# A layer of attention and gated FFN on one core: the softmax exponentials shared out anew between ScalarE and VectorE

## Chip, cores and metric

The kernel runs on one core of one Trainium2 chip. The metric is the device time of one execution in microseconds (us). Three runs of the kernel before gave 913.15, 915.69 and 915.77, a median of 915.69. One more execution was profiled. Where a statement rests on the profile, it is of that execution alone.

## What is computed

For x of 2048 rows and 640 columns: a layer norm, an attention with 32 heads of 20 columns without a mask, a residual, a second layer norm, a gated FFN of width 1728, and a second residual. Cut to what matters:

```python
def _A_ref(x, wqkv, wo):
    qkv = (x @ wqkv).reshape(B, S, 3, H, Dh).transpose(2, 0, 3, 1, 4)
    q, k, v = qkv[0], qkv[1], qkv[2]
    scores = jnp.einsum("bhqd,bhkd->bhqk", q, k) * (Dh ** -0.5)
    p = _softmax(scores, axis=-1)
    o = jnp.einsum("bhqk,bhkd->bhqd", p, v)
    return o.transpose(0, 2, 1, 3).reshape(B, S, D) @ wo

def _B_ref(x, w_gate, w_up, w_down):
    h = _gelu(x @ w_gate) * (x @ w_up)
    return h @ w_down

h  = x + _A_ref(_layernorm(x), A_wqkv, A_wo)
h2 = h + _B_ref(_layernorm(h), B_w_gate, B_w_up, B_w_down)
```

The scores are 32 x 2048 x 2048 numbers, and each needs one exponential.

## The kernel before

**Tiles, quads, slots.** A score tile is 128 keys by 512 queries' worth of one head (for chunks of fewer queries, several blocks of keys side by side), one bank of PSUM. Four heads stand in the four row groups of TensorE, so four tiles of the same keys make a quad. The queries are cut into eight chunks (CHUNKS) of 512, five times 256 and twice 128. A slot is 16 quads (64 tiles) of one chunk: chunk 0 has slots 0 to 7, chunks 1 to 5 have four slots each (8 to 27), chunks 6 and 7 two each (28 to 31). So there are 32 slots with 2048 tiles.

**Two engines for the exponential.** Most tiles go to ScalarE: units of alternately three and two tiles (PAT) are written by TensorE (score matmuls, L965), one ACTIVATE with the function Exp reads a unit from PSUM and writes its probabilities to a ring of 18 tiles (pts holds 12, pts2 in rege 6; both are the groups with line L368 on ACT). D_QUADS says, slot by slot, how many quads are computed by VectorE instead (d_exp): for each tile one TENSOR_SCALAR out of PSUM (L889), and then, for two tiles together (narrow, 128x1024) before slot D_WIDE = 18 and four together (wide, 128x2048) from there on, four operations that form a correction polynomial, a DMA issued by GpSimd that adds the correction into the tile (the slots in DA_SLOTS), and a last TENSOR_SCALAR. D_LEAD says how many ScalarE tiles ahead of its place in the slot a VectorE tile is begun.

**What follows a quad.** TensorE multiplies the probabilities with the values (PV, `ps<-pts,v_all` and like groups), adding up a slot in PSUM bank 6. The last PV of a slot waits for the slot's VectorE quads; then `osb` takes the sums out of the bank, and the next slot's PV begins there. ScalarE can't write a place of the ring before the PV that read it is done.

**Work between.** While the attention of chunk c + 1 runs, the output projection, the second layer norm and the FFN of chunk c (post, down) run in the gaps: L667 with wo, L1138 gate and up, L1218 down. DMA transposes on SyncE (dma_transposes) turn the normalised rows. The gelu of a chunk is on ScalarE, with a table load before and after. After the last Exp comes the tail: what is left of chunk 6, and all of chunk 7 after its attention.

**What sets the order.** The program is not written in its final order: `op` records operations with a planned duration, a latency after it (`lat`, for a DMA the time until it lands), a priority and dependencies. `Sched.schedule` then plays a list schedule and fixes the order of each engine's instructions; `emit` writes them with semaphore waits. Matmuls with zeros (`ps<-kt_all,zer`) are put in where the plan finds TensorE little used. So a changed count or latency moves instructions on all engines, though the work is the same. The constants in question:

```python
DA_ISSUE, DA_LAT = 0.95, 7.0
D_QUADS = (1,) + (2,) * 15 + (2, 2) + (3,) * 10 + (2, 2, 2, 2)
D_LEAD = ((0,) * 8, (0, 10, 20) + (42,) * 21)
D_WIDE = 18
```

Of the kernel before, what the change touches and what calls it, by code (L numbers as in the profile page):

```python
# [46 lines left out]
class Sched:  # L47
# [13 lines left out]
    def op(self, eng, fns, dur, prio, reads=(), writes=(), acq=(), rel=(), after=(), sem=None, lat=None, mode=None, util=0.0):  # L61
        if eng == "dve" and rel and prio > self.ev:
            prio = self.ev
        o = Op()
        o.i = len(self.ops)
        o.eng, o.dur, o.lat, o.sem = eng, dur, DRAIN[eng] if lat is None else lat, sem
        o.util = util
        o.mode = mode
        o.tag = writes[0] if writes else None
        o.fns = fns if isinstance(fns, list) else [fns]  # L70
        o.prio = (prio, o.i)
        deps = set(after)
        for r in reads:
            if r in self.lw:
                deps.add(self.lw[r])
        for w in writes:
            if w in self.lw:
                deps.add(self.lw[w])
            deps.update(self.rd.get(w, ()))
        for r in reads:  # L80
            self.rd.setdefault(r, []).append(o.i)
        for w in writes:
            self.lw[w] = o.i
            self.rd[w] = []
        deps.discard(o.i)
        o.deps = deps
        o.acq = list(acq)
        o.rel = list(rel)
        o.succ = []
        o.ready = 0.0  # L90
        self.ops.append(o)
        return o.i
# [237 lines left out]
PV_QUADS = 2  # L330
D_LAG = 8
MERGE = (1,)
DA_ISSUE, DA_LAT = 0.95, 7.0
DA_SLOTS = (1, 2, 3, 5) + tuple(range(9, 32))
PR, PR2 = 12, 6
D_QUADS = (1,) + (2,) * 15 + (2, 2) + (3,) * 10 + (2, 2, 2, 2)
D_FIRST, D_PART = 2, 0.75
D_LEAD = ((0,) * 8, (0, 10, 20) + (42,) * 21)
D_WIDE = 18
RSQRT_MAGIC = float(0x5F3759DF)  # L340

# [1 line left out]
P_QK, P_PV, P_PRO, P_EPI, P_LN, P_BG = 0, 1, 1.5, 2, 2.5, 3  # L343
# [3 lines left out]
def bass_sequential_preLN__mha_block__glu_gated_geglu__prompt_kernel(  # L347
# [12 lines left out]
    with ExitStack() as es:  # L360
        sc = Sched(nc)
        op = sc.op
# [4 lines left out]
        def I(method, *args, **kwargs):  # L367
            return lambda eng: getattr(eng, method)(*args, **kwargs)  # L368
# [64 lines left out]
        wg = carve(NA * DFF).rearrange("p (a f) -> p a f", a=NA)  # L433
        wu = carve(NA * DFF).rearrange("p (a f) -> p a f", a=NA)
# [55 lines left out]
        def cst(fn, key, n=128):  # L490
# [7 lines left out]
           reads=["zer"], writes=["qf1"])  # L498
        op("act", I("activation", f32(qt_all[:, 2, :, :]), zer[:, 0:2].bitcast(FP32).to_broadcast([128, 2048]), ACT.Copy), 1.8, P_QK,
           reads=["zer"], writes=["qf2"])  # L500
        op("act", I("activation", v_all[:, :, :, DH], zer[:, 0:1].unsqueeze(2).to_broadcast([128, NT, H]), ACT.Copy, bias=1.0), 0.5, P_QK,
           reads=["zer"], writes=["vones"])
# [28 lines left out]
        def load(dst, src, key, mb, after=(), writes=None):  # L531
            return op("sp", I("dma_start", dst, src), 0.08, P_BG, writes=writes or [key], after=after,
                      sem=key, lat=mb)
# [85 lines left out]
                   rel=[bk], after=after)  # L619

        def dma_transposes(src, rkeys, dst, wkey, after=()):
            op("sp", I("dma_start_transpose", dst, src), 1.25, P_EPI, reads=rkeys, writes=[wkey], sem=f"xp{wkey[1]}", lat=2.0, after=after)

        _id = [0]

# [114 lines left out]
        def proj_q(t, c, banks, prio, evac="dve"):  # L740
            proj_qk(0, t, c, q_un[:, t, :], ("qu", t), banks, prio, evac)
            if t == 0 and c == 0:
                for j in range(4):
                    q_keys[0][0].append(("q", 0, 0, j))
                    dma(qt_all[32 * j + 1:32 * j + 21, 0, 0, :], q_un[DH * j:DH * j + DH, 0, :], ("q", 0, 0, j),
                        [("qu", 0), "qtm0"], "qc", 2.2, prio - 0.1)
            dma(qdr[c, 128 * t:128 * t + 128, :], q_un[:, t, :], ("qdr", c, t), [("qu", t)], f"qw{t}", 2.7,
                max(prio, P_BG) if t == 0 else prio, 0.4)
            w_readers.append(op("dve", I("tensor_scalar", aq[t].bitcast(I16), q_un[:, t, :].bitcast(I16), 0x7FFF, None,
                                         ALU.bitwise_and), 0.2, prio, reads=[("qu", t)], writes=[aqk(t)]))  # L750

        def q_bound(c, ts, g0, g1, banks, prio):
            bk = Bank(*banks)
            key = ("bk", sc_id())
            for k, t in enumerate(ts):
                w_readers.append(op("pe", lambda eng, k=k, t=t: eng.matmul(
                    bank(bk)[0:32, :], sel[:, t, :], aq[t], start=(k == 0), stop=(k == len(ts) - 1)),
                    c_mm(512), prio, mode="full", util=0.05, reads=[aqk(t), ("sel", t)], writes=[key],
                    acq=[bk] if k == 0 else []))
            op("dve", lambda eng: eng.tensor_scalar(qoff[0:32, :], bank(bk)[0:32, :], OFF, None, ALU.add), c_dve(512), prio,  # L760
               reads=[key], writes=["qoff"], rel=[bk])
            dma(odr[c], qoff[0:32, :], ("odr", c, g0), ["qoff"], "ow", 2.5, prio, 0.4)
            new = [("qo", c, g0)] + [("q", c, g0, j) for j in range(4)]
            for j in range(4):
                dma(qt_all[32 * j + 1:32 * j + 21, c, g0:g1, :],
                    qdr[c].rearrange("(g j e) s -> j e g s", j=4, e=DH)[j, :, g0:g1, :], ("q", c, g0, j),
                    [("qdr", c, t) for t in ts] + q_fills[c], f"q{c}{g0}", 2.5, prio, keep=False)
            dma(qt_all[0:128:32, c, g0:g1, :], odr[c].rearrange("(g j) s -> j g s", j=4)[:, g0:g1, :], ("qo", c, g0),
                [("odr", c, g0)] + q_fills[c], f"q{c}{g0}", 2.5, prio, keep=False)
            for g in range(g0, g1):  # L770
                q_keys[g][c] += new
# [36 lines left out]
        slot_end = []  # L808
        lead = sum(D_LEAD, ())
        for s_, (c, gs) in enumerate(slots):  # L810
            nk = 512 // CHUNKS[c][1]
            quads = [(s_, g, kb) for g in gs for kb in range(NT // nk)]
            n = D_QUADS[s_]
            taken = [quads[len(quads) * (m + 1) // (n + 1)] for m in range(n)]
# [258 lines left out]
        def prefetch(c):  # L1073
            q0, nq = CHUNKS[c]
            nt = nq // 128
            tb = base(c)
            op("sp", I("dma_start", h_sb[:, tb:tb + nt, :], x_hbm[q0:q0 + nq, :].rearrange("(t p) d -> p t d", p=128)), 0.08, P_EPI,
               writes=[("h", tb + tt, hf) for tt in range(nt) for hf in range(2)], sem=f"xr{c}", lat=2.0 + nq * 0.0034,
               after=tuple(e_ops) + tuple(w_readers) if c == 0 else ())
# [167 lines left out]
        for s_, (c, gs) in enumerate(slots):  # L1247
            if c == 0:
                g = s_
                if g + 1 in STEP:  # L1250
                    t, (g0, g1) = g + 1, STEP[g + 1]
                    pr = P_EPI if t == 1 else P_BG
                    proj_q(t, 0, BG0, pr)
                    proj_k(t, BG0, pr)
                    q_bound(0, (t - 1, t), g0, g1, BG0, pr)
                if g < 3:
                    for kt in range(NT * g // 3, NT * (g + 1) // 3):
                        proj_v(kt, 1, BG0, P_BG)
                if g == 5:
                    prefetch(0)  # L1260
                if g >= 5:
                    cc = g - 4
                    for t in range(NA):
                        proj_q(t, cc, BG0, P_BG)
                    q_bound(cc, tuple(range(NA)), 0, NG, BG0, P_BG)
                if g == 7:
                    wr = tuple(w_readers)
                    load(wg, B_w_gate.rearrange("(a p) f -> p a f", p=128), "wg", 11.0, after=wr)
                    load(wu, B_w_up.rearrange("(a p) f -> p a f", p=128), "wu", 16.0, after=wr)
                    load(wd[:, 0:NF - 1, :], B_w_down[0:(NF - 1) * 128, :].rearrange("(a p) d -> p a d", p=128),  # L1270
                         "wd", 21.0, after=wr)
                    r0 = (NF - 1) * 128 - F0[-1]
                    load(wd[r0:128, NF - 1, :], B_w_down[(NF - 1) * 128:DFF, :], "wd", 2.6, after=wr)
                    op(POOL, I("memset", wd[0:r0, NF - 1, :], 0.0), 0.8, P_BG, writes=["wdz", "pool"], after=wr)
            while ui < len(units) and begins[ui] < slot_end[s_]:
                unit(ui)
                ui += 1
            if gs[-1] == NG - 1:
                tail = c == len(CHUNKS) - 1
                sc.ev = P_EV  # L1280
                post(c, ALLB if tail else BGF[c + 1], ALLB if tail else BGC[c + 1], tail)
                if not tail:
                    prefetch(c + 1)
# [30 lines left out]
```

## Time and profile before

| | us |
|---|---|
| device time, median of three | 915.69 |
| device time of the profiled execution | 915.13 |
| its span (first to last instruction) | 913.0 |
| ACT (ScalarE) busy | 871.2 |
| PE (TensorE) busy | 832.7 |
| DVE (VectorE) busy | 763.3 |
| POOL (GpSimd) busy | 134.2 |
| first and last Exp start | 32.9 and 875.2 |

The first 33 us are the loads, the first layer norm and the first projections; 33 to 876 us is the stretch of the exponentials, and the rest is the tail. Busy times overlap each other and an engine that is off the critical path may be busy or idle at no cost, so the table must be read with the chain of waits and, for each stage, with the windows. PE's busy time says little, since matmuls are pipelined and counted to their modelled end.

### The profile page before, as it was taken

What the parts mean: (1) busy time and instruction counts of PE and PEld (TensorE: products, weight loads), DVE (VectorE), ACT (ScalarE), POOL (GpSimd) and SP (SyncE); (2) the same over time, 40 slices, a digit from 0 to 9 for tenths busy, and PEclk for the clock granted to TensorE, in tenths of its full rate; (3) what the DMA queues carried; (4) which work ended last, traced back from release to release, by engine and by line L of the source; (5) the groups of instructions that cost most, each with busy time, mean ns of one, the idle gap of its engine ahead of it and who ended that gap; (6) DMA issues with size and microseconds to landing.
All of it is one profiled execution on the core that took longest, in us unless ns stands there. A gap on an engine that the chain in (4) does not pass through costs nothing.

```text
span 913.0 us, 25152 instructions
## 1 busy us (share of the span) xinstructions
PE 832.7 (91%) x11135; PEld 383.4 (42%) x11180; DVE 763.3 (84%) x1426; ACT 871.2 (95%) x786; POOL 134.2 (15%) x239
## 2 busy tenths in 40 slices
PE   3999999998897887899998989999999999999998
PEld 2432222222243332334443443344444445666667
DVE  8869989988798985777887989989999998958643
ACT  7999899999999999999999999999999999999971
POOL 5001110000013111111321101031102110203000
PEclk9999999999999999999999999999999999999999
DMA  7213344346304231242422324433353344314300
GB/s 259 84 31 79 79 87 108 96 96 203 127 1 76 48 59 24 48 68 59 91 51 50 64 39 85 91 62 71 78 107 62 70 81 98 47 26 85 56 9 23
DMA packets 52500, 68.05 MB, mean 75 GB/s; under 512 B 20892, under 2 KB 38392, under 8 KB 52392
## 3 DMA queue, kind: packets, MB, share of 16 engines
q0 software_dynamic: 12960, 33.56, 20.4%
q1 hardware_dynamic: 39432, 32.89, 13.2%
q8 instruction: 87, 1.43, 0.6%
q14 instruction: 21, 0.17, 0.1%
HBM read 20.12 MB, written 8.09 MB: 31 GB/s over the span
## 4 chain that ended last, share of the span: by engine, by line
ACT 68%; PE 19%; DVE 7%; DMA 2%; POOL 2%; issue 1%; SPq 0%
ACT pts L368 43%; ACT rege L368 24%; PE ps L965 5%; PE ps L667 4%; PE ps L1138 3%; PE ps L368 3%; PE ps L1218 3%; DMA regw<-in_A_wqkv_dram 1%; ACT L368 1%; DVE qt_all L368 1%; DVE rege L889 1%; DVE qt_all L889 1%; DVE dwx L368 1%; POOL nw L368 1%; DVE rege L368 1%
## 5 line engine op out<-in xcount | busy, mean ns | idle before, releaser
L368 ACT ACTIVATE pts<-ps 128x1536 bf16<-128x1536 f32 (+1 forms) x468 | 556.1, 1352 | 5.1 <-PE ps L965 2.7
L965 PE MATMUL ps<-qt_all,kt_all 32*128 32x256 bf16 (+2 forms) x4096 | 315.0, 274 | 42.6 <-ACT pts L368 25.5
L368 ACT ACTIVATE rege<-ps 128x1536 bf16<-128x1536 f32 (+1 forms) x232 | 289.7, 1359 | 5.5 <-PE ps L368 3.8
L965 PEld LDWEIGHTS ps<-qt_all,kt_all 32*128 32x128 bf16 x4096 | 108.6, 92 | 252.6 <-ACT pts L368 130.5
L1138 PE MATMUL ps<-rege,regw 128*128 128x256 bf16 (+2 forms) x1103 | 158.0, 274 | 9.6 <-DVE rege L1187 3.6
L368 PE MATMUL ps<-pts,v_all 128*21 128x256 bf16 (+2 forms) x2338 | 124.5, 276 | 0.4 <-ACT pts L368 0.3
L1138 PEld LDWEIGHTS ps<-rege,regw 128*128 128x128 bf16 x1120 | 85.9, 98 | 61.4 <-issue 27.0
L889 DVE TENSOR_SCALAR rege<-ps 128x512 int16<-128x512 f32 x120 | 82.3, 686 | 19.6 <-PE ps L965 18.7
L368 PE MATMUL ps<-rege,v_all 128*21 128x256 bf16 (+2 forms) x1358 | 91.8, 280 | 0.4 <-DVE rege L368 0.2
L889 DVE TENSOR_SCALAR qt_all<-ps 128x512 int16<-128x512 f32 x116 | 79.5, 686 | 12.0 <-PE ps L965 11.1
L667 PE MATMUL ps<-regw 128*128 128x512 bf16 (+1 forms) x345 | 84.2, 351 | 4.7 <-DMA regw<-in_A_wqkv_dram 1.6
L1218 PE MATMUL ps<-regw,rege 128*128 128x320 bf16 x448 | 78.1, 301 | 1.7 <-DVE rege L1222 0.8
L368 DVE TENSOR_TENSOR qt_all<-qt_all 128x2048 int16<-128x2048 f16 (+3 forms) x79 | 74.2, 940 | 1.0
L368 PEld LDWEIGHTS ps<-pts,v_all 128*21 128x21 bf16 x2338 | 53.9, 91 | 32.3 <-issue 26.9
L368 DVE TENSOR_SCALAR qt_all<-qt_all 128x2048 int16<-128x2048 int16 (+3 forms) x111 | 63.5, 574 | 1.0
L1187 DVE TENSOR_TENSOR rege<-rege,ps 128x512 bf16<-128x512 bf16 (+1 forms) x53 | 35.8, 678 | 23.7 <-PE ps L1138 21.8
L368 DVE TENSOR_TENSOR rege<-rege 128x1024 f16<-128x1024 f16 (+1 forms) x74 | 50.6, 684 | 0.9
L1218 PEld LDWEIGHTS ps<-regw,rege 128*128 128x128 bf16 x448 | 37.4, 97 | 30.5 <-issue 13.6
L368 DVE TENSOR_SCALAR rege<-rege 128x1024 int16<-128x1024 int16 (+2 forms) x112 | 48.3, 439 | 2.2 <-DMA rege<-qt_all 1.0
L368 PE MATMUL ps<-kt_all,zer 128*32 128x512 bf16 x576 | 49.5, 390 | 0.0
L667 PEld LDWEIGHTS ps<-regw 128*128 128x128 bf16 x360 | 28.1, 99 | 45.8 <-issue 24.4
L368 PEld LDWEIGHTS ps<-rege,v_all 128*21 128x21 bf16 x1358 | 36.0, 91 | 21.7 <-issue 14.2
(114 smaller groups left out, 785.4 us busy)
## 6 DMA issues: line engine op xcount, KB each, us to landing
qt_all<-qt_all POOLq DMA_DIRECT2D x11, 512.0 KB, 5.1
qt_all<-dwx POOLq DMA_DIRECT2D x11, 512.0 KB, 5.8
rege<-rege POOLq DMA_DIRECT2D x16, 256.0 KB, 3.6
rege<-dwx POOLq DMA_DIRECT2D x8, 512.0 KB, 5.3
dvx<-qt_all POOLq DMA_DIRECT2D x8, 512.0 KB, 4.6
rege<-in_A_x_dram SPq DMA_DIRECT2D x5, 640.0 KB, 5.8
q_rows<-regw SPq DMA_DIRECT2D x20, 128.0 KB, 1.9
out_dram<-rege SPq DMA_DIRECT2D x16, 160.0 KB, 2.6
```

Of the source, the lines that this page charges most:

```text
L368: return lambda eng: getattr(eng, method)(*args, **kwargs)
L667: yield op("pe", lambda eng, l=l, r=r, k=k: eng.matmul(bank(bk, n), l, r, start=(k == 0), stop=(k == len(steps) - 1)), c_mm(n) + cold, pri ...
L889: d_ops.append(op("dve", lambda eng: eng.tensor_scalar(v[:, 512 * h:512 * h + 512], bank(b), EXP_MUL, -32000.0, ALU.mult, ALU.max), c_dve( ...
L965: return lambda eng: eng.matmul(out()[:, kk * nq:(kk + 1) * nq], kt_all[32 * j:32 * j + 32, g, kt * 128:(kt + 1) * 128], qt_all[32 * j:32 ...
L1138: op("pe", lambda eng, a=a, f=f, fi=fi: eng.matmul(bank(bk)[:, fi * nq:(fi + 1) * nq], w[:, a, F0[f]:F0[f] + 128], hnT[:, a, 128 * tb:128 ...
L1187: hdone.append(op("dve", lambda eng, bu=bu, fv=fv, w=w: eng.tensor_tensor(fv, fv, bank(bu, w), ALU.mult), c_dve(w), p, reads=[ku] + hkeys( ...
L1218: op("pe", lambda eng, f=f, o=o, hf=hf, bk=bk: eng.matmul(bank(bk, 320), ha_f[:, o:o + 128], wd[:, f, hf * 320:(hf + 1) * 320], start=(f = ...
```

## The change

Four numbers of the schedule's input differ, and two tuples.

```diff
-DA_ISSUE, DA_LAT = 0.95, 7.0
+DA_ISSUE, DA_LAT = 0.95, 6.4
-D_QUADS = (1,) + (2,) * 15 + (2, 2) + (3,) * 10 + (2, 2, 2, 2)
+D_QUADS = (1,) + (2,) * 11 + (3, 2) * 3 + (3, 3, 2) * 3 + (3, 2, 3, 2, 2)
-D_LEAD = ((0,) * 8, (0, 10, 20) + (42,) * 21)
+D_LEAD = ((0,) * 8, (0, 10, 20) + (36,) * 21)
...
         def dma_transposes(src, rkeys, dst, wkey, after=()):
-            op("sp", I("dma_start_transpose", dst, src), 1.25, P_EPI, ..., lat=2.0, after=after)
+            op("sp", I("dma_start_transpose", dst, src), 1.25, P_EPI, ..., lat=2.8, after=after)
...
-                    load(wg, B_w_gate..., "wg", 11.0, after=wr)
-                    load(wu, B_w_up..., "wu", 16.0, after=wr)
+                    load(wg, B_w_gate..., "wg", 12.0, after=wr)
+                    load(wu, B_w_up..., "wu", 17.5, after=wr)
```

VectorE has 73 quads before and 74 after. Slots 12, 14, 16 and 29 have one more each, slots 20, 23 and 26 one less. VectorE tiles from slot 11 on are begun 36 ScalarE tiles ahead in place of 42. The schedule reckons the adding DMAs to land earlier (6.4 for 7.0, scaled by the size), and the DMA transposes and the weights of gate and up to land later. Every instruction's place is then set anew by the schedule.

## The prediction, as made before the changed kernel had run

> **What bounds the kernel now.** I read the busy times first, then the chain that ended last.
>
> ```profile
> PE 832.7 (91%) x11135; PEld 383.4 (42%) x11180; DVE 763.3 (84%) x1426; ACT 871.2 (95%) x786; POOL 134.2 (15%) x239
> ...
> ACT 68%; PE 19%; DVE 7%; DMA 2%; POOL 2%; issue 1%; SPq 0%
> ```
>
> ACT is nearly never idle, and the chain runs through it for 68%. In the view of the chain in order of time four Exps are 4.52 us and six are 6.78 us from start to start (60.93, 67.71, 74.49), so a pair of units, five tiles, takes 2.26 us: 0.452 us per tile. From 33 to 876 us time is ACT's work plus its idle gaps. I listed these gaps on ACT's timeline. Those that belong to low clocks are:
>
> ```profile
> 570.10 1.02 ACT L368 ACTIVATE pts<-ps 128x1024 bf16<-128x1024 f32 x1 [0.80 <-PE ps L965]
> 571.32 2.37 ACT L368 ACTIVATE pts<-ps 128x1536 bf16<-128x1536 f32 x2 [0.19 <-PE ps L965]
> ...
> 595.02 2.60 ACT L368 ACTIVATE rege<-ps 128x1536 bf16<-128x1536 f32 x2 [1.00 <-PE ps L965]
> 598.49 2.37 ACT L368 ACTIVATE pts<-ps 128x1536 bf16<-128x1536 f32 x2 [0.86 <-PE ps L965]
> ```
>
> The windows of 4 us there (columns PE, PEld, DVE, ACT, POOL busy, granted clock, DMA share, GB/s) show why scores came late:
>
> ```profile
> 564.00:568.00 4.00, 3.11 (x42) 1.36 (x44) 4.00 (x8) 4.00 (x5) 0.85 (x1) 0.87 0.01 4
> 568.00:572.00 4.00, 4.00 (x55) 1.29 (x43) 3.11 (x7) 3.00 (x3) 0.32 (x1) 0.70 0.80 143
> ...
> 588.00:592.00 4.00, 3.07 (x37) 1.07 (x37) 4.00 (x7) 4.00 (x5) 0.00 (x0) 0.86 0.02 4
> 592.00:596.00 4.00, 4.00 (x38) 1.62 (x36) 2.81 (x8) 3.00 (x3) 0.00 (x0) 0.50 0.00 0
> 596.00:600.00 4.00, 3.75 (x53) 1.94 (x53) 2.89 (x6) 3.01 (x4) 3.55 (x8) 0.79 0.26 50
> ```
>
> Twice TensorE has few matmuls (3.11 and 3.07 us busy of 4), and right after it the clock falls, to 0.50 in the worst window. Everywhere else between 33 us and the end the 25 us windows read 1.00. VectorE's load differs by stage:
>
> ```profile
> 350.00:375.00 25.00, 19.56 (x230) 7.25 (x231) 14.48 (x26) 24.97 (x22) 1.72 (x2) 1.00 0.19 32
> 450.00:475.00 25.00, 23.88 (x324) 11.61 (x312) 21.07 (x45) 25.00 (x24) 3.57 (x4) 1.00 0.34 68
> 600.00:625.00 25.00, 23.61 (x360) 10.58 (x360) 24.90 (x39) 24.94 (x23) 5.88 (x10) 1.00 0.37 71
> 675.00:700.00 25.00, 24.25 (x342) 10.97 (x340) 24.90 (x43) 24.99 (x24) 6.71 (x13) 1.00 0.23 44
> ```
>
> The third column of times is DVE: 14 to 21 us of 25 in slots 12 to 17, full in slots 18 to 27. Last, the end of the chain:
>
> ```profile
> 874.32 0.33 PE ps L965 x8
> 874.65 3.23 PE ps L1138 x32
> 877.87 0.56 PE ps L368 x32
> 878.43 0.16 PE ps L1138
> 878.59 1.92 PE ps L1218 x14
> ```
>
> After the last scores (L965) TensorE sets the pace to the end, with only short waits: 913.0 - 874.3 = 38.7 us. The last PV (L368, 877.87) could have begun when the last Exp ended (876.3); 32 matmuls of L1138 stood before it.
>
> **The change part by part.**
>
> *One quad more on VectorE.* Units: 700 before, 699 after (two fewer of three tiles, one more of two). ScalarE loses four tiles: 4 x 0.452 = **-1.81 us**, all on the path. VectorE gains, in the narrow form, 4 x 0.686 (L889) and per half quad 0.42 + 0.42 + 0.69 + 0.69 + 0.42, some 8.0 us a quad; wide, 2.74 + 0.69 + 0.69 + 1.22 + 1.22 + 0.69 = 7.25 us. Slots 12, 14, 16: +24 us where the windows from 350 to 500 us leave 35 us of DVE idle; slots 18 to 31: two wide quads fewer, -14.5 us. Cover: ACT's 1.0 us windows; gone where DVE has no idle left. GpSimd issues six narrow adding DMAs more and two wide ones fewer, about 0.9 us each: +3.6 us on an engine that is 15% busy, nothing on the path.
>
> *Two low clocks.* They cost ACT 0.80 + 0.19 and 1.00 + 0.13 + 0.86 = 2.98 us. Whether they return is read from the order. I counted the columns that TensorE streams in three successive score groups with all that stands between (three units are 3.4 us of ACT), matmuls on 32 rows or up to 32 columns at a quarter. The mean is 5430. In the order before, the two lowest places are 1662 (from unit 445) and 1918 (from 466), which are the two places above; the next, 2302 at unit 160, kept clock 1.00 in the trace. In the order after the lowest are 2302 (the same unit 160) and 2302 (unit 400). So nothing after is below what went unpunished before: **-2.98 us**, bounds 0 and -2.98.
>
> [...]
>
> *The tail.* The last gelu of chunk 5 stands 8 Exps before the last one in the order before, 16 before it after; what follows it moves ahead too. After the last score group the order has 32 matmuls of L1138 fewer (25 of 256 and 7 of 128 columns, those that stand ahead of the last PV), 109 of L1218 for 112, and 16 PV of a VectorE quad more. The 32 took 3.23 us: -3.23. Three of L1218 at 0.137 (1.92/14): -0.41. PV: +0.28 (0.56/2). Sum **-3.36 us**. It holds if the moved work finds room before the last scores: in both orders the last 20 units hold the same number of full matmuls (154 and 155). Bounds: 0 (no room, ACT waits instead) and -4.4 (the two waits of TensorE for DVE L1222 in the tail, 0.50 each, go as well).
>
> *Lead, DMA latencies, later transposes.* The trace can't show the new waits. ACT's gaps for PV (`PE ps L368`) and scores outside the above are 2.77, 0.42, 0.98, 0.66 and 1.05 us (at 95, 120, 199, 290, 302). The first three lie before the changed slots, and stay. The last two follow a late transpose (3.78 us on the chain at 285.79; the plan reckoned 1.25 + 2.0, now 1.25 + 2.8), and may go: down to -1.7. On the other side a VectorE quad is begun 36 x 0.452 = 16.3 us ahead for 19.0. Its own instructions after the last L889 are 4.5 us, and the DMA lands after 4.6 to 5.8 us (medians), at most 7.7: 10 to 13 us if DVE served it at once. One late landing costs 7.7 - 5.3 = 2.4 us. I take **+0.5**, near no change, since most places keep their distance; bounds -1.7 and +2.4. SyncE's queue has the same 181 issues in nearly the same order, and weights land at the time that was measured before (10.7 and 15.7 us), so later plans for them cost at most idle background work: 0.
>
> Sum: 913.0 - 1.81 - 2.98 - 3.36 + 0.5 = 905.4 us of span. Around the span lie 915.13 - 913.0 = 2.1 us: **907.5 us**. The profiled time is 0.6 below the median of the runs, 915.69; I don't correct for that.
>
> **Rivals.** [...]
>
> (b) *The tail's gain is only moved ahead*: for it, PE is 24 us busy of 25 in the last windows before 875; against it, the even number of full matmuls. Then 907.5 + 3.4 = 910.9.
>
> (c) *It does not do what it says*: VectorE's added 24 us in slots 12 to 17 leave 11 of 35 us idle, and the freed time comes back as ACT waits for PV. With -1.8 and half of the rest lost: 913 to 915.
>
> (d) *Slower: the shorter lead is too short.* One batch of the trace, from the last of its tiles to its last operation:
>
> ```profile
> 566.77 0.68 DVE L889 TENSOR_SCALAR rege<-ps 128x512 int16<-128x512 f32 x1
> ...
> 584.67 0.68 DVE L368 TENSOR_SCALAR rege<-rege 128x2048 int16<-128x2048 int16 x1
> ```
>
> took 585.35 - 566.77 = 18.6 us with DVE full: inside 19.0, but not inside 16.3. If so, the last PV of each of eight slots that keep three wide quads (18, 19, 21, 22, 24, 25, 27, 29) is 2.3 us late, the ring fills, ACT stops: 8 x 2.3 = 18.4, or 926 us. It decides from about 1.0 us of lateness a slot (8.2/8). Against: the chain is so long because DVE was full; slots 20, 23 and 26 now give it 7.25 us each, and a tile's own work is 10 to 13 us.
>
> **How the numbers follow.** Forecast 0.63, (a) 0.15, (b) 0.06, (c) 0.07, (d) 0.09. A measurement of this kernel tells about 0.3% from no change, here 2.7 us: faster is below 912.9, slower above 918.4. The forecast, (a) and (b) are faster, (c) counts as the same but for its lower end, (d) as slower but for mild cases: 0.83, 0.08, 0.09. The range is 904.0 to 912.5: low end from the bounds -1.7 and -4.0 (907.5 - 2.2 - 1.0 = 904.3), high end over (a) and (b) and 1.6 more for late landings; it leaves out (c) and (d).
>
> **What would show it.** Right: granted clock 1.00 in every window from 33 us on; 699 Exps, ACT's busy time near 871.2 - 1.8 = 869.4; from the last scores to the end near 35.3 us; the gaps of ACT from 350 to 870 us in sum under 1.5 us. Wrong: a window with 0.5 to 0.9 of clock (a); ACT gaps on L965 in the last 60 us (b); gaps for `PE ps L368` at the ends of slots from 12 on (c, d). DVE should be evenly loaded, 20 to 24 us in each 25 from 350 to 800.

## The result and the profile after

| kernel | executions | device time, us | ratio to before | profiled span, us | mean granted clock |
|---|---|---|---|---|---|
| before | 20 | 914.33 (912.45 to 916.16) | | 913.0 | 0.994 |
| after | 20 | 917.82 (912.88 to 919.98) | 1.0028 [1.0017, 1.0040] | 917.9 | 0.983 |

The changed kernel is no faster; the median says 0.28% slower, at the edge of what this measurement can tell. Its executions fall in two groups: 15 of 20 have a span of 915.2 to 917.9 us at a clock of 0.981 to 0.987, five have 910.8 to 911.3 us at 0.991 to 0.993. The profiled one (919.98 us of device time) belongs to the first group.

The page of the kernel after: busy times, the granted clock in 40 slices, and the chain that ended last.

```profile
PE 839.0 (91%) x11176; PEld 386.4 (42%) x11222; DVE 772.0 (84%) x1450; ACT 870.5 (95%) x785; POOL 134.6 (15%) x243
...
PEclk9999999999999999999999599999999999999999
...
ACT 58%; PE 31%; DVE 7%; POOL 2%; issue 1%; DMA 1%
```

ACT's share of the chain fell from 68 to 58% and PE's rose from 19 to 31%, but these shares are no measure of the waits: ACT's gaps among the exponentials grew by 9.3 us, 1% of the span (table below), and the kernel with 24 fills in section 2, 6.6 us faster than this one, reads ACT 56% and PE 32%. The digit 5 in the clock's row is one slice, 23 us long, in which the granted clock was 0.50 from 509 us on. The windows of 4 us there and at two other places (columns PE, PEld, DVE, ACT, POOL busy, granted clock, DMA share, GB/s):

```profile
448.00:452.00 4.00, 2.44 (x45) 1.10 (x40) 3.93 (x10) 3.03 (x4) 0.00 (x0) 0.91 0.78 144
...
504.00:508.00 4.00, 3.02 (x46) 1.24 (x42) 4.00 (x6) 4.00 (x5) 0.86 (x1) 1.00 0.01 2
508.00:512.00 4.00, 3.93 (x42) 1.39 (x43) 3.84 (x6) 3.80 (x5) 0.00 (x0) 0.67 0.70 135
512.00:516.00 4.00, 4.00 (x40) 1.76 (x40) 1.93 (x3) 2.40 (x2) 0.00 (x0) 0.50 0.00 0
516.00:520.00 4.00, 4.00 (x40) 1.25 (x41) 2.11 (x5) 2.88 (x3) 0.85 (x1) 0.50 0.68 131
...
856.00:860.00 4.00, 1.69 (x48) 1.11 (x38) 1.57 (x4) 3.98 (x4) 0.00 (x0) 1.00 0.38 52
860.00:864.00 4.00, 4.00 (x89) 3.58 (x87) 0.69 (x1) 3.98 (x3) 0.00 (x0) 0.61 0.02 4
```

Each time a window with little matmul work (2.44, 3.02, 1.69 us busy of 4) comes first and the low clock follows. At 504 us TensorE has nothing but scores, PV and a few zero matmuls; its timeline shows no L1138 or L1218 between them. At 857 us there is also a wait: TensorE stood idle for 1.94 us until a DMA transpose had landed (last line).

```profile
504.89 0.39 PE L965 MATMUL ps<-qt_all,kt_all 32*128 32x256 bf16 x6
...
505.34 0.49 PE L368 MATMUL ps<-pts,v_all 128*21 128x256 bf16 x10
505.81 0.61 PE L965 MATMUL ps<-qt_all,kt_all 32*128 32x256 bf16 x6
507.15 0.61 PE L965 MATMUL ps<-qt_all,kt_all 32*128 32x256 bf16 x8 [0.73 <-ACT rege L368]
...
859.74 0.96 PE L1138 MATMUL ps<-rege,regw 128*128 128x128 bf16 x14 [1.94 <-DMA rege<-o_nat]
```

From 512 us on PE reads 4.00 busy and does less: 40 matmuls in a window for 46 at 504. So a fall of the clock can't be seen in the busy time. ACT's timeline in the same stretch shows the price (in brackets the idle time ahead of the first, and what ended it):

```profile
514.28 1.45 ACT L368 ACTIVATE rege<-ps 128x1536 bf16<-128x1536 f32 x1 [1.33 <-PE ps L965]
516.20 1.02 ACT L368 ACTIVATE rege<-ps 128x1024 bf16<-128x1024 f32 x1 [0.47 <-PE ps L965]
518.14 2.36 ACT L368 ACTIVATE pts<-ps 128x1536 bf16<-128x1536 f32 x2 [0.92 <-PE ps L965]
522.23 2.52 ACT L368 ACTIVATE pts<-ps 128x1536 bf16<-128x1536 f32 x2 [1.73 <-PE ps L965]
526.22 1.45 ACT L368 ACTIVATE rege<-ps 128x1536 bf16<-128x1536 f32 x1 [1.47 <-PE ps L965]
...
649.82 2.37 ACT L368 ACTIVATE pts<-ps 128x1536 bf16<-128x1536 f32 x2 [1.26 <-PE ps L368]
...
869.26 3.28 ACT L368 ACTIVATE pts<-ps 128x1024 bf16<-128x1024 f32 x3 [2.30 <-PE ps L965]
```

To see where the time went I split both spans at the first and the last Exp:

| part of the span, us | before | after | difference |
|---|---|---|---|
| up to the first Exp | 32.86 | 32.99 | +0.1 |
| Exps, table loads, gelu, start to start without gaps | 831.95 | 831.08 | -0.9 |
| gaps of ACT beside low clocks | 2.98 | 11.84 | +8.9 |
| all other gaps of ACT | 7.39 | 7.80 | +0.4 |
| start of the last Exp to the end | 37.80 | 34.15 | -3.6 |

The 11.84 us are 6.76 at 510 to 529, 2.14 at 450 to 455, 0.64 at 572 to 574 and 2.30 at 867.

### The profile page after: what moved, and what is told of

Same layout as the page of the kernel before. It is cut to its first block, busy times and chain, and to the rows that moved or that the text cites. A ratio compares the mean times of both kernels' runs of the same rounds, so it can differ in the third digit from the quotient of the medians.

```text
span 917.9 us, 25276 instructions
## 1 busy us (share of the span) xinstructions
PE 839.0 (91%) x11176; PEld 386.4 (42%) x11222; DVE 772.0 (84%) x1450; ACT 870.5 (95%) x785; POOL 134.6 (15%) x243
## 4 chain that ended last, share of the span: by engine, by line
ACT 58%; PE 31%; DVE 7%; POOL 2%; issue 1%; DMA 1%
ACT pts L368 36%; ACT rege L368 20%; PE ps L965 9%; PE ps L368 6%; PE ps L1138 5%; PE ps L667 5%; PE ps L1218 4%; DVE dwx L368 1%; DVE qt_all L368 1%; ACT L368 1%; DVE rege L889 1%; DVE qt_all L889 1%; PE ps L1057 1%; DMA rege<-o_nat 1%; POOL nw L368 1%
## 5 line engine op out<-in xcount | busy, mean ns | idle before, releaser
L1138 PE MATMUL ps<-rege,regw 128*128 128x256 bf16 (+2 forms) x1103 | 156.7, 276 | 10.9 <-DVE rege L1187 2.9
L1138 PEld LDWEIGHTS ps<-rege,regw 128*128 128x128 bf16 x1120 | 87.2, 99 | 60.3 <-issue 29.7
L889 DVE TENSOR_SCALAR rege<-ps 128x512 int16<-128x512 f32 x124 | 84.7, 684 | 18.8 <-PE ps L965 17.4
L1218 PE MATMUL ps<-regw,rege 128*128 128x320 bf16 x448 | 81.2, 305 | 2.6 <-DVE rege L1222 1.6
L368 DVE TENSOR_TENSOR qt_all<-qt_all 128x1024 int16<-128x1024 f16 (+3 forms) x83 | 75.6, 911 | 1.1
L368 PE MATMUL ps<-kt_all,zer 128*32 128x512 bf16 x624 | 56.4, 400 | 0.0
L1218 PEld LDWEIGHTS ps<-regw,rege 128*128 128x128 bf16 x448 | 37.9, 98 | 33.8 <-issue 15.5
L889 DVE TENSOR_SCALAR dvx<-ps 128x512 int16<-128x512 f32 x56 | 38.4, 685 | 11.6 <-PE ps L965 11.2
```

What stands on the lines that cost most here:

```text
L889: d_ops.append(op("dve", lambda eng: eng.tensor_scalar(v[:, 512 * h:512 * h + 512], bank(b), EXP_MUL, -32000.0, ALU.mult, ALU.max), c_dve( ...
L1138: op("pe", lambda eng, a=a, f=f, fi=fi: eng.matmul(bank(bk)[:, fi * nq:(fi + 1) * nq], w[:, a, F0[f]:F0[f] + 128], hnT[:, a, 128 * tb:128 ...
L1218: op("pe", lambda eng, f=f, o=o, hf=hf, bk=bk: eng.matmul(bank(bk, 320), ha_f[:, o:o + 128], wd[:, f, hf * 320:(hf + 1) * 320], start=(f = ...
```

## The experiments

A *fill* here is a throwaway matmul, 128x128 weights on 512 columns, written into a unit's own score bank just ahead of its scores, which overwrite it. It adds TensorE work; the order of all else stays. The edit, with FILL naming the units:

```diff
-RSQRT_MAGIC = float(0x5F3759DF)
+RSQRT_MAGIC = float(0x5F3759DF); FILL = {...}
...
-            qk = op("pe", fns, 0.222, P_QK, ...
+            qk = op("pe", [I("matmul", PS[:, 512 * s0:512 * s0 + 512], kt_all[:, 0, 0:128], kt_all[:, 0, 0:512], start=True, stop=True, skip_group_check=True)] * FILL.get(u, 0) + fns, 0.222, P_QK, ...
```

From the dearer form on, a fill of one or two stands ahead of two-tile units alone, also where a stretch of units is named. "Ratio" is always to the kernel before in the same set, with its 95% interval.

**1. Is it the low clock? Fills in the lean stretches.**

`FILL`: one in units 346-357, 398-416, 441-446, eight at 683.

> The changed kernel, with one matmul of throwaway data (128x128 by 512 columns into the unit's own score bank, which the scores then overwrite) ahead of the score matmuls in 37 units around the four places where the clock fell, and eight ahead of unit 683 at the last gelu but one. Order and work of all other engines are the same. Theory clock (low TensorE use halves the clock, and the slow scores make ACT wait): the granted clock stays at 1.00 at 451, 509, 571 and 861 us, the ACT gaps of 11.8 us there shrink to under 2, median 906 to 909. Rival lead (VectorE quads begun too late, quads badly placed): ACT's gaps remain with the clock at 1.00, median 915 to 919. Rival fill: the extra matmuls delay scores, so that it is slower than 918.

Measured: 915.13 us, ratio 1.0015 [1.0007, 1.0024]; the clock was 1.0 in six of 11 executions and 0.996 or more in all. The time expected was missed. The filled places stayed at full clock (the profiled execution, with a mean clock of 0.996, had two short falls elsewhere, at 348 and 829 us), and the gap at 867 us fell from 2.30 to 0.58, but in the filled stretches ACT had new gaps of 0.30 to 0.67 us ahead of Exps of three tiles (446 to 455, 510 to 522).

`FILL` in the kernel before: one in units 442-452 and 462-474.

> The kernel before with one such matmul ahead of the scores in units 442 to 452 and 462 to 474, the two places where its clock fell. Theory clock: 1.00 throughout, about 3 us faster than before, 910.5 to 912.5. If the low clock costs nothing of its own: 914 to 915.

Measured: 917.81 us, ratio 1.0059 [1.0038, 1.0080]. The profiled execution had clock 1.0 and a span of 914.2, where the kernel before at clock 1.0 has 910.4: this form costs 3 to 4 us by itself. Neither of the two times expected came. Three of the 12 executions had spans of 922.0 to 922.3 us at a clock of 0.987 to 0.991; they have no trace, so where their clock fell isn't known.

The control, in the kernel after: one in units 300-311, 470-488, 590-603, away from the lean stretches.

> Control: the changed kernel with the same matmul ahead of the scores of 45 units (300 to 311, 470 to 488, 590 to 603), where its clock was 1.00. Theory clock: times as of the changed kernel, in two groups near 913 and 918, median 917 to 919, the clock falls at the same places. If the extra matmuls helped in some other way: under 913.

Measured: 925.77 us, ratio 1.0134 [1.0117, 1.0150]. The clock fell at 452, 513 (17 us) and 868 us, the three places of the kernel after. It is slower than either time expected. So these fills, away from the lean stretches, cured none of the three, and one ahead of every unit cost several us (925.77 for 917.82).

A dearer form, two ahead of two-tile units, in the kernel after (151-157, 164-168, 346-357, 398-417, 441-446, 656-665; four at 267, 268, 439, 440, eight at 683) and before (118-124, 164-168, 218-223, 444-453, 463-476, 544-550):

> The changed kernel with two throwaway matmuls ahead of the scores of two-tile units alone (whose scores have the 1.33 us of a three-tile Exp to come in), in six stretches around its lean places (units 151 to 157, 164 to 168, 346 to 357, 398 to 417, 441 to 446, 656 to 665), and four to eight before the scores that wait for a gelu (267, 268, 439, 440, 683). Order of all else unchanged. Theory clock: 1.00 nearly throughout, and without the delays that the first form of the fill put ahead of three-tile Exps (0.3 to 0.7 us each, some 4 us): span 905 to 908, median 907 to 910. Rival (the changed order is no better at the full clock than the one before): span 910.4 or more, median over 912.5.

> The kernel before with the same form of fill in units 118 to 124, 164 to 168, 218 to 223, 444 to 453, 463 to 476 and 544 to 550. Theory clock: its fast runs with clock 1.00 had a span of 410 less noise, that is 910.4; this gives 910 to 911.5 in nearly all runs, median 912.3 to 913.7. Rival (the fill always costs more than it saves): over 914.5.

Measured: 917.13 us, ratio 1.0034 [1.0021, 1.0047], and 919.93 us, ratio 1.0062 [1.0049, 1.0075]. Both kept clock 1.0 in all five executions, and neither gained: both misses in time. In the kernel after the fill left 2.2 us of gaps between 510 and 536 us alone. These runs alone don't exclude the rival that was named for the first: an order that is no better at full clock.

**2. The mild form.** One fill ahead of the two-tile units between 398 and 417, ten matmuls, at the long fall alone; then one in 346-357 and eight at 683 besides, 24 in all.

> The kernel after, with one throwaway full matmul (128x128 on 512 columns, into the unit's own score bank) ahead of the scores of the two-tile units between units 398 and 417 alone, 10 matmuls in all. If the low clock from 509 to 530 us is what parts most executions of the kernel after (span 915.2 to 917.9) from the five quick ones (910.8 to 911.3), every execution now has a span near 911 and a clock of 0.991 or more: device time 912.5 to 914, median near 913.2. If the low clock is only a sign of scores that are late for another reason, or if ten fills cost as much as they save, the median stays at 916 to 918.

> As the run before, and one such matmul ahead of the two-tile units from 346 to 357 and eight ahead of unit 683 as well, 24 matmuls in all. The falls at 451 and 861 us should go with that at 509: the gaps of ACT there, 2.14 and 2.30 in the kernel after, shrink to about 0.6 each. If low clocks are the cause: 910 to 912 of device time at a clock of 0.996 or more. If fills cost what they save: 913.5 to 916.

Measured: **912.05 us, ratio 0.9971 [0.9961, 0.9982]**, nine executions with spans of 909.3 to 910.5, no second group; and **911.22 us, ratio 0.9962 [0.9949, 0.9975]**, spans 907.8 to 909.5 at a clock of 0.998 to 1.0. Both have the clock that was expected, and both beat the two kernels, though by less than 1% of the time. The first is a little quicker than expected; the second is within 910 to 912, with a gap of 0.59 us at 860 as expected, but 1.19 us in four gaps from 450 to 458, where about 0.6 was expected. The second one's windows (columns as above):

```profile
504.00:508.00 4.00, 3.51 (x50) 1.50 (x48) 4.00 (x6) 4.00 (x5) 0.85 (x1) 1.00 0.00 2
508.00:512.00 4.00, 4.00 (x53) 1.59 (x55) 3.63 (x6) 3.92 (x4) 0.00 (x0) 1.00 0.71 135
512.00:516.00 4.00, 4.00 (x64) 1.80 (x60) 3.60 (x7) 3.82 (x4) 0.85 (x1) 1.00 0.00 0
516.00:520.00 4.00, 4.00 (x60) 1.79 (x59) 3.72 (x6) 3.65 (x4) 0.00 (x0) 1.00 0.71 135
```

Its ACT timeline, the two gaps left in this stretch and the one that answers to 867 us:

```profile
517.81 2.37 ACT L368 ACTIVATE pts<-ps 128x1536 bf16<-128x1536 f32 x2 [0.35 <-PE ps L965]
520.41 2.36 ACT L368 ACTIVATE rege<-ps 128x1536 bf16<-128x1536 f32 x2 [0.24 <-PE ps L965]
...
860.38 3.28 ACT L368 ACTIVATE pts<-ps 128x1024 bf16<-128x1024 f32 x3 [0.59 <-PE ps L965]
```

At clock 1.00 the same stretch does 60 and 64 matmuls in a window for 40, and ACT loses 0.59 us in it for 6.76. The ten matmuls of the first of the two kernels took 5.8 us off the median (917.82 to 912.05). Its profiled execution (clock 0.994) still has falls of 3.4 us at 348, 451 and 854 us, so what the ten removed is the long one: the fall at 509 us is the cause of the first group's time.

The counterpart in the kernel before: one ahead of two-tile units in 444-452 and 471-474, two in 465-470.

> The kernel before with the mild form of the fill at its own two lean stretches: ahead of the two-tile units one throwaway matmul in units 444 to 452 and 471 to 474, two in units 465 to 470, 12 to 13 matmuls in all. It is the counterpart of the kernel after with few fills (911.22). If the change itself is worth something once neither kernel has low clocks, this one stays above it: its clock is 1.0 in most executions, it saves the 1 to 3 us of the falls and pays about 1.2 us of small gaps, so 913 to 914.5. If the fills alone made 911.2, it comes to 911 to 912 too, and the change is worth nothing at full clock.

Measured: 914.49 us, ratio 1.0019 [1.0002, 1.0036]; eight of 12 executions had clock 1.0, with spans of 911.5 to 912.8, median 911.75. It stays above the kernel after with few fills, as expected of a change that is worth something: 911.75 - 909.1 (median of the five spans there) = 2.6 us. Two things limit this figure. The other four executions had spans of 914.0 to 918.5 us at 0.991 to 0.998, with falls that no trace shows. And without any fill the kernel before had 910.3 to 910.7 us in its six executions at clock 1.0, only 1.4 us above 909.1; so its fills cost it some 1.2 us.

**3. Is it the zero matmuls?** The kernel before without them in the attention (576 fell to 133):

```diff
-                        for fn in o.fns:
+                        for fn in (o.fns[:1] if o.tag == "warm" else [f for f in o.fns if f not in self.pad]):
```

> The kernel before with its padding matmuls cut from 576 to 133 (of each four with zeros one or none is kept), the order of all else unchanged. What is left out adds zeros. Theory clock: the clock falls at many more places (mean granted clock 0.96 to 0.985), and the kernel is 8 to 30 us slower. Rival (padding only takes TensorE's time): same or faster, 905 to 914.

Measured: 914.37 us, ratio 1.0003 [0.9992, 1.0013], clock 0.994 to 0.998 in all ten executions. A plain miss: these matmuls aren't what holds the clock of the kernel before.

**4. Which part of the change?** Only the latencies (6.4, 2.8, 12.0, 17.5) in the kernel before; then the change without them (7.0, 2.0, 11.0, 16.0 put back); then the lead alone in the kernel before:

```diff
-D_LEAD = ((0,) * 8, (0, 10, 20) + (42,) * 21)
+D_LEAD = ((0,) * 8, (0, 10, 20) + (36,) * 21)
```

> The kernel before with only the assumed latencies of the change (adding DMAs 6.4, transposes 2.8, weights 12.0 and 17.5): the same work, quads and lead, another order. Theory clock: the time moves by the low clocks that this order happens to have, and by ACT's gaps there; its order has lean stretches near 70% and 81 to 84% of the exponentials, so two to three falls and 913 to 919. Rival latencies (a later assumed landing is itself worth something): 911 to 913 with the clock as before.

> The changed quads and lead with the latencies of before (adding DMAs 7.0, transposes 2.0, weights 11.0 and 16.0): ACT's work as in the changed kernel, another order. Theory clock: its time is given by the low clocks that this order has; with one fall at most 907 to 911, each further fall 1 to 3 us. Rival latencies (the order suffers from landings that are assumed too early): more waits for transposes, 915 or more.

> The kernel before with only the shorter lead (36 for 42 tiles), its quads and latencies unchanged. If the shorter lead is too short in some slots (rival d of the prediction, in a mild form), ACT has new gaps of 1 to 5 us that end with PV (PE L368) at ends of slots from 12 on, and the time is 916 to 920. If the lead is harmless, no gap over 0.5 us ends with PV after 350 us, and the time is 913 to 915.5 where the order leaves TensorE no new lean stretch.

Measured: 930.21 us, ratio 1.0161 [1.0127, 1.0196]; 915.60 us, ratio 1.0020 [1.0008, 1.0031]; 922.49 us, ratio 1.0090 [1.0073, 1.0108]. The first and the third are slower than either time expected.

The latencies alone: half clock for 23.9 us from 588.5 on, again after a window with PE 3.00 us busy of 4.

```profile
584.00:588.00 4.00, 3.00 (x47) 1.60 (x45) 3.97 (x7) 4.00 (x4) 0.00 (x0) 1.00 1.00 190
588.00:592.00 4.00, 3.24 (x23) 0.88 (x23) 1.06 (x2) 1.80 (x3) 0.00 (x0) 0.56 0.14 52
```

The profiled execution (span 923.0, clock 0.985) is one of the quicker of six; the middle ones have 928.1 to 928.3 at 0.976 and no trace.

The change without them: clock 0.996 to 1.0 in all ten executions, and no fall longer than 3.4 us in the profiled one (0.998). Both ways round it is the latencies, that is the order that follows from them, that bring the long falls. Which of the four numbers does it I didn't try, nor the quads alone. The time expected there (907 to 911) was missed, by one place. The chain in order of time shows ACT's last Exp before a gap of 4.65 us, and what stood ahead of the PV that ended it:

```profile
531.50 1.35 ACT rege L368
532.85 0.05 issue
532.90 0.39 PE ps L965 x6
533.29 2.07 PE ps L1138 x18
535.36 0.33 PE ps L368 x8
535.69 1.20 PE ps L1138 x10
536.89 0.57 PE ps L368 x16
537.47 0.02 issue
537.49 1.02 ACT rege L368
```

TensorE isn't idle here: 28 matmuls of L1138 (3.27 us) stand in its order between the scores and the PV that frees the ring. Without that gap the span of 913.8 would be about 909.

The lead alone: two gaps of 3.08 and 3.22 us that end with PV, as rival (d) had it. The chain at the second:

```profile
670.03 1.22 DVE qt_all L368
671.26 0.61 DVE osb L368
671.87 0.04 issue
671.91 0.65 PE ps L368 x16
672.56 0.02 issue
672.58 1.45 ACT pts L368
```

VectorE runs nearly without a break (busy 9.73 us of the 10 from 662 on), `osb` comes late in its queue, the next slot's PV after it, and the ring is full. The clock is not the cause: it was 0.998 in four of the five executions, and in the profiled one (0.994) the gaps beside its short falls are 3.6 us more. In the kernel after, with its quads and latencies, the same lead gave one such gap of 1.26 us (649.82 above).

## Why the prediction was wrong

**The step that failed** is the one on the low clocks: "So nothing after is below what went unpunished before: -2.98 us". Measured in its place: +8.9 us (2.98 to 11.84 us of gaps). The term is off by 11.8 us, and 917.9 - 905.4 = 12.5 us is the whole error of the span. Two things in it were wrong:

*The count doesn't tell which place will fall.* Units 160 and 400 had the same lowest count, 2302, and unit 160 had gone unpunished in the one trace I had. In the trace of after it went unpunished again (windows of 4 us from 220 to 232 us: PE 3.37, 2.69 and 3.17 us busy, clock 1.00), while at unit 400, at 505 us, the clock fell for 20.5 us after a window with 3.02 us busy. So neither the count nor the busy time parts the two, and what does is not shown. The weights in the count (32 rows or up to 32 columns at a quarter) were a choice of mine that no run here tests.

Nor does one place fare alike in every execution. From 344 to 348 us PE is 2.45 us busy in the trace of after, and the clock stayed at 1.00; it fell at 348 us in the profiled executions of the first set of fills and of the ten fills (sections 1 and 2), whose order up to there is that of the kernel after. Of the 20 executions of the kernel after 15 had the longer time; where the clock fell in those without a trace isn't known. The count had found the place at 504 us and couldn't say whether it would fall. It named none of the other three falls (5.08 of the 11.84 us), and that at 861 us it could hardly see: an order doesn't tell how long TensorE will wait for a transpose, here 1.94 us.

*One fall was long.* Case (a), a window with 0.5 to 0.9 of clock, is what came; it had a chance of 0.15 and a place in the range, up to 912.5. The two falls of the kernel before had lasted 3.4 and 6.8 us and cost 0.99 and 1.99 us of gaps; in the kernel after three lasted 3.4 us and the one at 509 us 20.5 us. At half clock the stretch there does 40 matmuls in 4 us where it does 60 in the kernel with 24 fills. That the fall held itself, since the slow scores kept TensorE's work low, is my estimate and not shown: the ten fills stand along the whole stretch, and no run has them at its start alone. The fall alone cost 6.8 us of gaps in the profiled execution.

**A quad less on ScalarE**, -1.81: the right size. 699 Exps. By the table they take, start to start, 0.9 us less in the kernel after, and by the same measure some 1.5 less in the kernel with ten fills (about 830.5); in the kernel after more Exps stand behind a gap, where one of three tiles takes 1.45 us, and in a row 1.33.

**The tail**, -3.36: right. From the last scores (883.31) to the end it is 34.6 us for 38.7, -4.1, within the bounds; from the start of the last Exp, -3.6. What stands there now, for the 32 matmuls of L1138 before:

```profile
883.31 0.33 PE ps L965 x12
883.64 0.33 PE ps L368 x16
883.97 1.60 PE ps L1218 x11
```

**Lead, latencies, transposes**, +0.5: right for this kernel, +0.4. It is a sum of both signs: the gaps at 290 and 302 shrank from 1.71 to 0.41, as held possible; that at 198 grew from 0.98 to 1.72 with a smaller one beside it gone, and 1.26 at 649 is new. But that it came out so near to "near no change, since most places keep their distance" was luck: the lead alone costs 6.3 us in two slots, and the latencies alone 16 us.

**Rivals.** (b) fell: the tail's gain stayed, and ACT's gap near the end (2.30) went to 0.59 with the clock. (c) fell: VectorE is busy 20.0 to 23.4 us of each 25 from 350 to 500, as intended. (d) is real and mild: one slot here, two with the lead alone, at about 3.1 us where I had put 2.3 in each of eight.

At nearly full clock the change is worth 1.4 to 2.6 us (section 2: against the kernel before without and with fills), for 1.81 + 3.36 - 0.5 = 4.7 forecast without the clock's term. With the fills there are gaps in both kernels (2.2 us at the filled places of the one, 1.6 us new ones in the other), so the figure is rough.

One slip in the prediction's sums: the "-4.0" from which the range's low end is worked out stands for the tail's bound of -4.4; the low end itself goes by -4.4.

## What to carry to other kernels

Where an order leaves TensorE little work, don't rely on how low a count gets: of two places with 2302 columns one fell here and one didn't. A stretch that went unpunished in one trace is no proof, and several executions with their clocks say more than one profile. A handful of throwaway matmuls at the lean place, ahead of the units whose scores have the longer Exp to come in, can be worth more than the change itself (5.8 us here). Put ahead of every unit, they gave back more than half of that in the kernel after (915.1 for 912.1) and cost the kernel before more than they mended (ratio 1.0059). When a number of a scheduler's input is changed, price the new order and not the number: the lead alone made this kernel 0.9% slower and the latencies alone 1.6%, through stretches that no sum of operations shows.

## What the runs showed of the hardware that was not expected

- Low clock without long idleness: ahead of the fall at 509 us TensorE was busy 3.02 us of 4, and the longest idle piece in the timeline there was 0.73 us; ahead of the two falls of the kernel before, with 3.11 and 3.07 us busy, the longest were 0.52 and 0.93 us.
- One program, two times: the kernel after takes 911 or 916 us of span, and the mean clock (0.991 to 0.993, or 0.981 to 0.987) tells which.
- Without 443 of 576 zero matmuls the time was the same (1.0003), and the clock was 0.994 to 0.998, for 0.992 to 0.998 in the kernel before of the same set. The reason stays open.
- In the kernel after, the DMA transpose ahead of the lean window at 856 us took 6.42 us from issue to the matmul that waited for it, where the order reckons 1.25 + 2.8:

```profile
853.28 6.42 DMA rege<-o_nat
859.74 0.96 PE ps L1138 x14
```
